# FFN2 of the second half as seven block products for eight of eighteen tile pairs, with attention's pieces dealt anew

## The chip, the cores and the metric

The kernel runs on one core of one Trainium2 chip. The metric is the device time of one execution in microseconds; each kernel is executed several times and the median counts. Five engines matter: PE (TensorE, matmuls, with PEld for its weight loads), DVE (VectorE), ACT (ScalarE), POOL (GpSimd) and SP (SyncE). In this kernel SP, ACT and POOL issue the DMA transfers.

## The reference

```
xn  = layernorm(x)                                   # x: 2048 tokens x 576
q, k, v = split(xn @ wqkv)                           # 32 heads of 18
attn[s, w] = softmax over w of q[s] . k[s - 2 w] / sqrt(18),   w = 0..7, s - 2 w >= 0
A   = (sum over w of attn[s, w] * v[s - 2 w]) @ wo
h   = relu(xn @ w1 + b1) ** 2                        # 4608 wide
B   = h @ w2 + b2
out = x + A + B                                      # all in fp32
```

## The kernel before, in words

**Tiles.** The 2048 tokens are four blocks b = 0 to 3 of 512. The 4608 columns of the hidden layer are 36 tiles of 128, taken in 18 pairs p. The 576 output features are five chunks, four of 128 and one of 64. Everything lies transposed: features in the partitions, tokens along the free axis.

**Precision.** An fp32 operand is split into a rounded part ("hi", written by ACT) and the rest ("lo", written by DVE), and a product is hi·hi + lo·hi + hi·lo. One tile of FFN2 in one block is 14 matmuls of 512 columns (`tile_products`, `add`): four chunks times three, and two for the chunk of 64, where hi and lo lie side by side. ACT therefore writes `w2s` (hi of w2) and `h` (hi), and DVE writes the lo of both, for every tile or pair.

**Stages.** `phase_a(0)` computes FFN1 of blocks 0 and 1 together, pair after pair (`ffn_pair`), by seven block products in Strassen's manner (the slots are named T1, B11, B22, B21, T3, T2, T4; `S1` to `S4` are sums of blocks of xn). Between its matmuls stand those of FFN2 of block 0. The squared hidden values of block 1 are stored in DRAM (`hscr`). `phase_b0` is FFN2 of block 1 from there, and then q, k and v of the second half ("quads", L1093). `phase_a(1)` and `phase_b1` do for blocks 2 and 3 what the first two did for 0 and 1. `tail` closes block 3. At the end of each block come five steps with `wo` (`o_ops`), whose operand is attention's output, loaded by `regroup` (`st<-o`, `r<-o`), transposed and split by `o_hi` and `o_lo`.

**Attention** runs on DVE, ACT and POOL beside the matmuls. A group of heads of a block is a generator of 19 pieces: four products with k and their four reductions in turn, the maximum, the exponential, sum and division, then four products with v and their four sums in turn. `side(k)` puts k pieces at the place in the program where it is called; `complete(b)` puts all that are left up to block b. Eight such generators run in the second half.

**Order.** Every engine executes its instructions in the order in which the code is written; the same holds for the three DMA queues. A piece of attention that stands ahead of a drain or a split on DVE is done first.

**What to look for.** FFN1's matmuls are at L661 and L667, FFN2's at L557; `w2_hi` at L530, `h_hi` at L989; `drain` adds a finished bank to the residual; all two-operand VectorE work goes through `tt`, L118 (L128 in the changed kernel). In the changed kernel FFN2's matmuls are at L590, those of the block products at L1514, `w2_hi` at L562, `o_hi` at L1011 and L1012, the sum and division of attention at L416 and L417.

Of the kernel before, what the change touches and what calls it, by code (L numbers as in the profile page):

```python
# [45 lines left out]
PIECES = (0, 0, 0, 2, 3, 4, 0, 3, 1, 0, 2, 2, 1, 0, 2, 2, 4, 5)  # L46
# [4 lines left out]
def block_kernel(ctx: ExitStack, tc: tile.TileContext, x, xt, wqkv, wo, w1, b1, w2, b2, w1l, out):  # L51
# [55 lines left out]
    lwscr = [dram.tile([G, 2, L, NS * P], F32, name=f"lw{i}") for i in range(-(-NP // G))]  # L107
    hscr = [[dram.tile([P, 2 * TB], F32, name=f"h{s}{p}") for p in range(NP)] for s in range(2)]
# [246 lines left out]
    def fetch():  # L355
        while free[0] > kept_back[0] and loads:
# [6 lines left out]
            t = landed[kind, b, g] = kv_tile(NE * CG + 32)[:, :NE * CG].rearrange("p (e c) -> p e c", c=CG)  # L363
            if kind == "k":
# [3 lines left out]
            lane[0].dma_start(t.rearrange("p e c -> p (e c)"),  # L368
                              flat(scr[kind][g], (PAD + b * TB - HALO) * CG, [NJ * CG, P], NE * CG))
# [58 lines left out]
    current = [None, None, None]  # L428

    def side(k, exp=True):  # L430

        while k > 0:
            if current[0] is None:
# [3 lines left out]
                current[:] = [make(), None, name]  # L437
            if current[1] == "exp" and not exp:
                return k
            try:  # L440
                current[1] = next(current[0])
                k -= 1
            except StopIteration:
                current[0] = None
        return 0

# [43 lines left out]
    def open_w1(n, k):  # L490
        w1s[n, k] = mt.tile([P, 2, 4, 2 * P], F32R, name="w1s", bufs=3)[:, :, :slots(n, k)]
# [18 lines left out]
    stream = [(b, n) for b in range(NB) for n in (*range(NF), *(f"o{c}" for c in range(NC)))]  # L510
# [11 lines left out]
    his, los = [0], [0]  # L522
# [9 lines left out]
    def w2_lo():  # L532
# [6 lines left out]
        load_w2(i + 3)  # L539
# [98 lines left out]
    def ffn_pair(s, p, work, first=False):  # L638
# [5 lines left out]
        stacked = p >= PLAIN  # L644
        A11 = lambda k, c: X[b0][:, k, c]
# [8 lines left out]
        def product(to, slot, a, start=False):  # L654
# [3 lines left out]
            if stacked:  # L658
                mm.append((LW[p % 2, slot], ST[slot]))
# [9 lines left out]
        def part(i):  # L669
# [9 lines left out]
            if i == 0 and p + 1 >= PLAIN and not last:  # L679
                load_left_weights(p + 1)  # L680
            if i == 0 and p == 1 and s:
                load_stack(1, sb.tile([P, 4, TB], F32R, name="w1r", bufs=2), 4)
# [33 lines left out]

        def finish_pair():
# [11 lines left out]
        if current[1] == "exp":  # L729
# [8 lines left out]
        if not first:  # L738
            side(2 + (p > 2) if s else PIECES[p], False)
# [10 lines left out]
        if before:  # L750
            next(before, None)

        def splits():
# [4 lines left out]
            if not own_w2:  # L758
# [3 lines left out]
            if not own_w2:  # L762
# [14 lines left out]
        elif not last:  # L777
            w1_hi(n + 1, 1)
            w1_lo(n + 1, 1)
        product(ba, B21, A12)  # L780
# [3 lines left out]
        work(2)  # L784

        def third():
            product(bc, B22, S4)
            left(bc, 1, x4["d"])
            if not first:
                part(1)  # L790
                side(2)
# [17 lines left out]
        else:  # L809
            third()  # L810
            h0 = square_hi(r0)
            square(r0)
            fourth()
        side(2, False)
        hs[n] = h0
        prev["r"] = r0, r1, h0
        prev["finish"] = finish_pair()
        work(3)

    def phase_a(s, filler):  # L820
# [3 lines left out]
        for p in range(1, NP):  # L824
            h, ops = hs.pop(s * NP + p - 1), []

            def work(i):
                if i in (0, 2):
                    ops.extend(tile_products(b, 2 * p - 2 + i // 2, h))
                add(b, ops[7 * i:7 * i + 7])  # L830

            if p == NP - 1:
# [7 lines left out]
        if s:  # L840
            residual(b)
        else:
# [5 lines left out]
        load_h(s, 0)  # L848
# [17 lines left out]
        load_h(s, 1)  # L866
        load_left(b)
        for c in range(NC):
            w2_hi()
            if c == 2:  # L870
                h_hi(s, 0)
            add(b, o_ops(b, c), range(NC) if c == NC - 1 else ())
# [7 lines left out]
        finish(b)  # L880
# [3 lines left out]
    def regroup(b, k):  # L884
        if b == 1:
            assert free[0]
# [913 lines left out]
```

## Time and profile before

| | us |
| --- | --- |
| median of 3 runs | 1105.33 (1104.26 to 1106.77) |
| the profiled execution | 1104.88 |
| its span | 1103.2 |
| TensorE granted clock | 1.0 in every stage |

The profiled execution is one of those runs, 0.4 us below their median; 1.7 us of it lie outside the span. The stages in the trace: `phase_a(0)` to about 430, `phase_b0` to about 660 (the quads in its last third), `phase_a(1)` to about 970, `phase_b1` and `tail` to the end.

### The profile page before, as it was taken

The page shows a single profiled execution, that of the slowest core. Times are in us where ns is not written, and L with a number is a line of the kernel's source. Part 1 is how long each engine was busy: PE and PEld are TensorE (multiplying, and loading weights), DVE is VectorE, ACT ScalarE, POOL GpSimd, SP SyncE. Part 2 cuts the span into 40 slices and gives each one's busy share as a digit, 9 for nine tenths or more (in the row PEclk, how much of TensorE's full clock was granted, in tenths as well). Part 3 has the DMA queues.
Part 4 walks back from the last instruction along what each step waited for, and adds up shares of the span by engine and source line. Part 5 has one row for each costly group of instructions (what it writes and reads, how often), then busy time and mean ns, then how long its engine had stood idle before and what let it go on. Part 6 is the DMA issues. An engine that isn't in the chain of part 4 may idle for free.

```text
span 1103.2 us, 13965 instructions
## 1 busy us (share of the span) xinstructions
PE 1091.4 (99%) x4919; PEld 918.8 (83%) x4919; DVE 889.3 (81%) x1197; ACT 566.5 (51%) x801; POOL 156.8 (14%) x284
## 2 busy tenths in 40 slices
PE   9999999999999999999999999999999999999998
PEld 7998888888888888888899887888888888888887
DVE  7996888999988979989899285776867676889955
ACT  5555655666656564555344354454554545543432
POOL 4011220212130100003010300202101010101010
PEclk9999999999999999999999999999999999999999
DMA  8768998897898697876865988868686877685582
GB/s 275 260 210 294 307 362 305 315 379 275 316 349 297 227 383 245 289 241 226 311 193 164 314 307 278 283 239 320 216 308 209 295 236 301 227 282 190 184 284 87
DMA packets 106549, 297.32 MB, mean 270 GB/s; under 512 B 12784, under 2 KB 39664, under 8 KB 95728
## 3 DMA queue, kind: packets, MB, share of 16 engines
q1 hardware_dynamic: 69104, 188.26, 49.1%
q0 software_dynamic: 14272, 67.24, 17.2%
q10 hardware_dynamic: 23104, 40.94, 11.1%
q8 instruction: 38, 0.62, 0.2%
q14 instruction: 31, 0.25, 0.1%
HBM read 211.90 MB, written 84.49 MB: 269 GB/s over the span
## 4 chain that ended last, share of the span: by engine, by line
PE 88%; DVE 6%; DMA 2%; issue 2%; ACT 1%; ACTq 1%; POOL 0%; DVEq 0%; POOLq 0%
PE p L557 45%; PE p L661 34%; PE p L1093 4%; DVE pr L118 2%; DMA w1s<-w 1%; PE p L1465 1%; PE p L1555 1%; PE p L1097 1%; DVE h L118 1%; DMA out<-h 1%; PE p L667 1%; PE p L1610 1%; DVE r L118 0%; PE p L1382 0%; DVE w1s L118 0%
## 5 line engine op out<-in xcount | busy, mean ns | idle before, releaser
L557 PE MATMUL p<-h,w2s 128*128 128x512 f32 x2066 | 491.9, 389 | 0.0
L557 PEld LDWEIGHTS p<-h,w2s 128*128 128x128 f32 x2066 | 387.6, 188 | 81.7 <-ACT h L708 0.5
L661 PE MATMUL p<-X,w1s 128*128 128x512 f32 x864 | 219.3, 389 | 0.0
L530 ACT ACTIVATE w2s<-w2r 128x640 fp32r<-128x640 f32 x164 | 120.3, 736 | 139.4 <-PE p L557 108.1
L661 PEld LDWEIGHTS p<-X,w1s 128*128 128x128 f32 x864 | 162.2, 188 | 33.7
L118 DVE TENSOR_TENSOR w2s<-w2r,w2s 128x576 fp32r<-128x576 f32 (+1 forms) x165 | 124.0, 752 | 77.2 <-ACT w2s L530 77.1
L661 PE MATMUL p<-S,w1s 128*128 128x512 f32 x648 | 164.8, 390 | 1.4 <-ACT r L746 1.4
L661 PEld LDWEIGHTS p<-S,w1s 128*128 128x128 f32 x648 | 121.5, 188 | 27.2 <-ACT r L746 1.8
L424 POOL DMA_DIRECT2D o<-q x128 | 69.5, 613 | 422.9 <-DVE q L118 421.8
L704 ACT ACTIVATE r<-r,b1t 128x512 f32<-128x512 f32 x72 | 52.2, 724 | 116.3 <-DVE r L118 113.6
L118 DVE TENSOR_TENSOR pr<-lg,kv 128x1152 f32<-128x1152 f32 x64 | 86.7, 1355 | 1.1
L395 DVE TENSOR_REDUCE lg<-pr 128x64 f32<-128x1152 f32 x64 | 86.5, 1351 | 1.2
L118 DVE TENSOR_TENSOR pr<-q,kv 128x1152 f32<-128x1152 f32 x64 | 86.7, 1354 | 0.9
L118 DVE TENSOR_TENSOR r<-p,r 128x512 f32<-128x512 f32 (+1 forms) x77 | 53.1, 690 | 35.5 <-ACT r L770 17.3
L118 DVE TENSOR_TENSOR pr<-pr 128x576 f32<-128x576 f32 (+1 forms) x128 | 77.6, 606 | 3.3
L712 ACT ACTIVATE r<-r 128x1024 f32<-128x1024 f32 x72 | 76.1, 1056 | 1.2
L746 ACT ACTIVATE r<-p 128x512 f32<-128x512 f32 x36 | 21.5, 598 | 84.2 <-PE p L661 81.1
L118 DVE TENSOR_TENSOR h<-r,h 128x1024 fp32r<-128x1024 f32 (+2 forms) x43 | 49.8, 1162 | 13.4 <-ACT r L712 9.6
L118 DVE TENSOR_TENSOR w1s<-w1r,w1s 128x1024 fp32r<-128x1024 f32 (+2 forms) x42 | 46.3, 1103 | 8.7 <-ACT w1s L495 8.2
L704 ACT ACTIVATE r<-p,b1t 128x512 f32<-128x512 f32 x72 | 48.2, 671 | 0.4 <-DMA out<-r 0.4
L118 DVE TENSOR_TENSOR h<-h 128x1024 fp32r<-128x1024 f32 x36 | 43.9, 1220 | 1.7 <-ACT h L989 1.5
L557 PE MATMUL p<-w1s,w2s 128*128 128x512 f32 x195 | 44.7, 389 | 0.0
(227 smaller groups left out, 1185.1 us busy)
## 6 DMA issues: line engine op xcount, KB each, us to landing
w2r<-in_w SPq DMA_DIRECT2D x144, 320.0 KB, 3.7
kv<-kvq POOLq DMA_DIRECT2D x32, 1296.0 KB, 8.2
w<-w1s SPq DMA_DIRECT2D x21, 1024.0 KB, 6.6
w1s<-w ACTq DMA_DIRECT2D x19, 1024.0 KB, 6.2
h<-r SPq DMA_DIRECT2D x36, 512.0 KB, 6.1
h<-h SPq DMA_DIRECT2D x36, 512.0 KB, 4.3
w<-w1s SPq DMA_DIRECT2D x15, 768.0 KB, 9.6
w1s<-w ACTq DMA_DIRECT2D x15, 768.0 KB, 5.6
```

The lines of the kernel that those rows point to most:

```text
L118: return nc.vector.tensor_tensor(out=out, in0=a, in1=b, op=op)
L395: nc.vector.tensor_reduce(out=lg[:, j * HG:(j + 1) * HG].rearrange("p a w -> p w a"), in_=pr.rearrange("p w (a d) -> p w a d", d=DH), axis ...
L424: nc.gpsimd.dma_start(rows[:, i], q[i * L:(i + 1) * L, :, a:z])
L530: nc.scalar.activation(w2s[stream[i]][:, :DE], raw2[i], AF.Copy)
L557: nc.tensor.matmul(yp[b][c], v, a, start=c not in yb[b], stop=c in last and c not in [o[0] for o in ops[i + 1:]], skip_group_check=True)
L661: nc.tensor.matmul(to, l, r, start=start and i == 0, stop=i == len(mm) - 1, skip_group_check=True)
L667: nc.tensor.matmul(to, weight(LEFT, k, f), v, start=False, stop=k == 1, skip_group_check=True)
L704: nc.scalar.activation(to, a, AF.Relu, bias=b1t[:, f:f + 1])
L712: nc.scalar.activation(r, r, AF.Square)
L746: nc.scalar.activation(u[:, 0], bb, AF.Copy)
L1093: nc.tensor.matmul(to, l[:, js], r, start=start and n == 0, stop=n == len(mm) - 1, skip_group_check=True)
L1097: nc.tensor.matmul(to, v[:, js], ws[LEFT, f][:, n], start=False, stop=n == 1, skip_group_check=True)
```

## The change

For the eight odd pairs 1, 3, ..., 15 (`PAIRED`), FFN2 of blocks 2 and 3 is done for both blocks at once by seven block products. The two-by-two blocks are: the two tiles of a pair against the two token blocks for h, and the two tiles against two halves of four chunks for w2.

- In `phase_a(1)` a paired pair isn't multiplied by w2. `finish_paired` forms its seven operands (squares and their sums and differences) and stores them in DRAM (`opscr`, 1.79 MB a pair). The matmuls of FFN2 of block 2 that remain, two tiles of ten pairs, are spread: one tile (14 matmuls) for each pair of FFN1 instead of two.
- A new `phase_blocks`, ahead of FFN2 of block 3, has 28 steps (`ORDER`). A step loads one operand of 512 KB, splits it two steps ahead, and does 12 matmuls, or 16 where the chunk of 64 goes along. The weights of the eight pairs come in four quadrants (`w2q`), are subtracted from each other in place (`turn_weights`) and split (`weights_hi`, `weights_lo`). Sums of banks go to the residual in between.
- FFN2 of block 3 has 20 tiles left: 18 in a loop, then five steps with wo, then two in `tail`.
- Attention's pieces are dealt by tables of numbers: `QUADS` in the quads, `SPOTS` in `phase_a(1)`, `LAST` in `phase_blocks`, `SINGLES` in the loop of block 3, one digit or count for each place.
- Left-over weights of FFN1 (`load_left_weights`) come two pairs ahead instead of one; the stack of left-over rows is loaded in pair 1 instead of in the quads; buffers for block 1's and block 3's attention output and residual change; k is loaded ahead of q.

```diff
+SPOTS = ('000001',) + ('110022', '110023', '110023', '110023') * 4 + ('110021',)
+QUADS = ('01111110111110', '10100010101011', '00110111111111', '10010000111111', ...)
+LAST = '0000000000000000001111111111'
+SINGLES = '12121212121200000000'
+PAIRED = tuple(range(1, 16, 2))
...
+        def finish_paired():
+            r1, t = prev.pop("r")
+            k = PAIRED.index(p)
+            y = mt.tile([P, 4, TB], F32, name="h", bufs=3)
+            nc.scalar.activation(y[:, :2], r1, AF.Square)
+            tt(t[:, 2], y[:, 0], y[:, 1], ALU.add)
+            tt(t[:, 3], t[:, 2], t[:, 0], ALU.subtract)
+            yield
+            nc.sync.dma_start(opscr[k // 2][:, k % 2, :4], t)
+            tt(y[:, 2], t[:, 1], t[:, 3], ALU.subtract)
+            tt(y[:, 0], t[:, 0], y[:, 0], ALU.subtract)
+            nc.sync.dma_start(opscr[k // 2][:, k % 2, 4:], y[:, :3])
+            yield
...
-                if n in ((1, 2, 3, 4, 5, 6, 8, 9, 10, 11, 12), (0, 2, 5, 6, 8, 10, 12, 13), (2, 3, 5, 6, 7, 8, 9, 10, 11, 12, 13), (0, 3))[2 * k + half]:
-                    side(1)
+                side(int(QUADS[2 * k + half][n]))
...
+    ORDER = ([(B11, A11S, g) for g in range(NG)] + [(T1, S1S, g) for g in range(NG)] +
+             [(T2, S2S, g) for g in range(NG)] + [(B21, A12S, g) for g in range(NG // 2)] +
+             [(T3, S3S, g) for g in range(NG)] + [(B21, A12S, g) for g in range(NG // 2, NG)] +
+             [(B22, S4S, g) for g in range(NG)] + [(T4, A22S, g) for g in range(NG)])
...
+    WHEN = {1: [(T1, 1)], 3: [(T2, 0)], 5: [(T2, 1)], 6: [(B21, 0)], 8: [(B21, 1)], 10: [(T3, 0)],
+            12: [(T3, 1)], 16: [(B22, 0)], 18: [(B22, 1)], 20: [(T4, 0)], 22: [(T4, 1)]}
...
+            operand_hi(k + 2)
+            for at in WHEN.get(k, ()):
+                weights_hi(*at)
+            operand_lo(k + 2)
+            for at in WHEN.get(k, ()):
+                weights_lo(*at)
...
+            if k == 19:
+                for c in range(2):
+                    tt(x2[:, c], aa[c], x2[:, c], ALU.add)
...
+            side(int(LAST[k]))
...
+                if len(xr[b]) < 2 and (m == 12 or not queue and current[0] is None):
+                    complete(b)
+                    regroup(b, 0)
+                    regroup(b, 1)
...
+                for c in {14: (0,), 15: (1,), 16: (2,), 17: (3,)}.get(m, ()):
+                    o_hi(b, c)
+                    o_lo(b, c)
+                side(int(SINGLES[m]))
```

**Where instructions move, 1.** VectorE of the changed kernel, from what follows step 19 of `phase_blocks` in the code to the end of step 20. The names: `S_7717<-p` adds banks to the residual of block 2, `xf` is the chunk of 64, `sm` and `lg` are a softmax piece, `X` is a weight quadrant turned, `h` the lo of operand 22 and `w1s` that of 21 and 23, `w1r` the lo of T4's weights.

```order
L128 TENSOR_TENSOR w1s<-w1s 128x1024
L128 TENSOR_TENSOR S_7717<-p_7900,S_7717 128x512
L128 TENSOR_TENSOR S_7717<-p_7901,S_7717 128x512
L1063 SCALAR_TENSOR_TENSOR xf<-p_5712,b2t,xf 64x512
L128 TENSOR_TENSOR xf<-p_5712,xf 64x512
L416 TENSOR_REDUCE sm<-lg 128x32
L417 RECIPROCAL sm<-sm 128x32
L128 TENSOR_TENSOR lg<-lg,sm 128x256
L128 TENSOR_TENSOR X_7719<-X_7719 128x1024
L128 TENSOR_TENSOR h<-h 128x1024
L128 TENSOR_TENSOR w1r<-X_7719,w1r 128x1024
L128 TENSOR_TENSOR pr<-lg,kv 128x1152
```

Before, FFN2 of block 3 stood here; three tiles of it put these rows on VectorE, with three pieces of attention (a product, its reduction, the maximum):

```order
L118 TENSOR_TENSOR h<-h 128x1024
L118 TENSOR_TENSOR pr<-q,kv 128x1152
L118 TENSOR_TENSOR w2s<-w2r,w2s 128x576
L395 TENSOR_REDUCE lg<-pr 128x8x8
L401 TENSOR_REDUCE mx<-lg 128x32
L118 TENSOR_TENSOR lg<-lg,mx 128x256
L118 TENSOR_TENSOR w2s<-w2r,w2s 128x576
L118 TENSOR_TENSOR h<-h 128x1024
```

The drains, the piece, the turn and the two splits now stand in one run, where one split of 576 or 1024 stood between pieces.

**Where instructions move, 2.** VectorE in FFN2 of block 3, from the last sums of attention (`q<-pr` is its output) to the first transposes for wo (`STREAM_TRANSPOSE`), before:

```order
L118 TENSOR_TENSOR q<-pr 128x144
L118 TENSOR_TENSOR w2s<-w2r,w2s 128x576 x2
L118 TENSOR_TENSOR h<-h 128x1024
L118 TENSOR_TENSOR w2s<-w2r,w2s 128x576 x2
L118 TENSOR_TENSOR h<-h 128x1024
L118 TENSOR_TENSOR w2s<-w2r,w2s 128x576 x2
L118 TENSOR_TENSOR h<-h 128x1024
L118 TENSOR_TENSOR w2s<-w2r,w2s 128x576 x2
L118 TENSOR_TENSOR h<-h 128x1024
L916 STREAM_TRANSPOSE r_8914<-st 128x512
```

and with the change:

```order
L128 TENSOR_TENSOR q<-pr 128x144
L128 TENSOR_TENSOR w2s<-w2r,w2s 128x576 x2
L128 TENSOR_TENSOR h<-h 128x1024
L1011 STREAM_TRANSPOSE r_8905<-st 128x512
L128 TENSOR_TENSOR w1s<-r_8905,w1s 128x512
L128 TENSOR_TENSOR w2s<-w2r,w2s 128x576
L1011 STREAM_TRANSPOSE r_8928<-st 128x512
L128 TENSOR_TENSOR w1s<-r_8928,w1s 128x512
L128 TENSOR_TENSOR w2s<-w2r,w2s 128x576
L128 TENSOR_TENSOR h<-h 128x1024
```

Eight tiles (one `w2s` each) lay between the last sum and the first transpose; two lie there now.

## Rows read from the trace of the kernel before

**Rows 1.** The page: the span, then each engine's busy time, share and instructions.
```profile
span 1103.2 us, 13965 instructions
...
PE 1091.4 (99%) x4919; PEld 918.8 (83%) x4919; DVE 889.3 (81%) x1197; ACT 566.5 (51%) x801; POOL 156.8 (14%) x284
```

**Rows 2.** Windows: stretch and us, then each engine busy, granted clock, DMA share, GB/s.
```profile
core 0: us, PE busy (x) PEld busy (x) DVE busy (x) ACT busy (x) POOL busy (x), PEclk, DMA share, GB/s
100.00:400.00 300.00, 299.96 (x1320) 247.30 (x1319) 265.86 (x384) 187.08 (x252) 58.29 (x100) 1.00 0.87 316
...
500.00:700.00 200.00, 194.44 (x906) 169.59 (x905) 153.34 (x198) 87.91 (x137) 29.38 (x53) 1.00 0.78 256
700.00:950.00 250.00, 250.00 (x1104) 207.09 (x1103) 175.80 (x217) 128.45 (x177) 28.31 (x53) 1.00 0.74 262
```

**Rows 3.** PE's timeline in FFN2 of block 3: start, us, instruction, count.
```profile
1035.81 36.43 PE L557 MATMUL p<-h,w2s 128*128 128x512 f32 x160
```

**Rows 4.** Timelines of 563 to 577, the quads; in brackets idle before and its releaser.
```profile
571.69 1.35 DVE L395 TENSOR_REDUCE lg<-pr 128x64 f32<-128x1152 f32 x1
572.95 1.05 DVE L118 TENSOR_TENSOR w1r<-w1r 128x864 f32<-128x864 f32 x1
...
574.03 0.92 ACT L1025 ACTIVATE w1s<-w1r 128x864 fp32r<-128x864 f32 x1 [3.28 <-DVE w1r L118]
574.87 0.94 ACT L1103 ACTIVATE kv<-p 128x432 f32<-128x432 f32 x2
...
575.43 1.08 PEld L1093 LDWEIGHTS p<-h,X 128*128 128x128 f32 x6 [1.28 <-ACT kv L1103]
```

**Rows 5.** DVE's timeline of 649 to 672, the end of block 1 and after.
```profile
650.01 2.48 DVE L118 TENSOR_TENSOR h<-p,h 128x512 f32<-128x512 f32 x4
652.41 1.40 DVE L118 TENSOR_TENSOR r<-p,r 64x512 f32<-64x512 f32 x2
...
668.98 0.41 DVE L406 TENSOR_REDUCE sm<-lg 128x32 f32<-128x256 f32 x1
...
670.27 1.36 DVE L118 TENSOR_TENSOR pr<-lg,kv 128x1152 f32<-128x1152 f32 x1
```

**Rows 6.** DVE's timeline of 1040 to 1049.5, the last pieces of attention.
```profile
1043.42 0.75 DVE L118 TENSOR_TENSOR w2s<-w2r,w2s 128x576 fp32r<-128x576 f32 x1
1044.09 1.22 DVE L118 TENSOR_TENSOR h<-h 128x1024 fp32r<-128x1024 f32 x1
1045.22 1.25 DVE L118 TENSOR_TENSOR pr<-pr 128x576 f32<-128x576 f32 x2
1046.50 0.31 DVE L118 TENSOR_TENSOR q<-pr 128x144 f32<-128x144 f32 x1
1046.73 1.42 DVE L118 TENSOR_TENSOR w2s<-w2r,w2s 128x576 fp32r<-128x576 f32 x2
```

**Rows 7.** POOL's timeline of 1036 to 1072: the stores of attention's output and `regroup`.
```profile
1047.11 4.33 POOL L424 DMA_DIRECT2D o<-q  x8 [35.86 <-DVE q L118]
1054.22 0.56 POOL L899 DMA_DIRECT2D st<-o  x1 [2.78 <-DMA o<-q]
```

**Rows 8.** DMA issues of 1040 to 1080: KB each and median us to landing.
```profile
h<-h SPq DMA_DIRECT2D x5, 512.0 KB, 4.8
...
st<-o POOLq DMA_DIRECT2D x1, 768.0 KB, 7.6
...
o<-q POOLq DMA_DIRECT2D x4, 48.0 KB, 4.0
```

**Rows 9.** Timelines of DVE and ACT where the first chunk for wo is transposed and split.
```profile
1068.34 0.70 DVE L916 STREAM_TRANSPOSE r<-st 128x512 f32<-128x512 f32 x1
...
1069.08 0.63 ACT L917 ACTIVATE w1s<-r 128x512 fp32r<-128x512 f32 x1 [1.91 <-DVE r L916]
1069.61 0.72 ACT L530 ACTIVATE w2s<-w2r 128x640 fp32r<-128x640 f32 x1
```

**Rows 10.** The chain that ended last (start, us), and PE's timeline at its end.
```profile
659.73 15.16 DMA w1s<-w
...
674.93 0.72 PE L667 MATMUL p<-x,w1s 128*128 128x512 f32 x2 [1.73 <-DMA w1s<-w]
```

**Rows 11.** DMA issues of 700 to 950: KB each and median us to landing.
```profile
w1s<-w ACTq DMA_DIRECT2D x13, 1024.0 KB, 5.5
...
st<-o POOLq DMA_DIRECT2D x1, 768.0 KB, 13.9
```

**Rows 12.** The page: DMA busy tenths and GB/s in 40 equal slices of the span.
```profile
DMA  8768998897898697876865988868686877685582
GB/s 275 260 210 294 307 362 305 315 379 275 316 349 297 227 383 245 289 241 226 311 193 164 314 307 278 283 239 320 216 308 209 295 236 301 227 282 190 184 284 87
```

More of the change, by code (lines that the diff above doesn't have):

```diff
@@ L445, in side, with some_side @@
         return 0
+    owed = [0]
+    def some_side(t):
+        owed[0] += t
+        while True:
+            exp = current[1] == "exp"
+            cost = COST[steps_done[0]] if current[0] is not None else COST[0]
+            if owed[0] < cost / 2 or side(1):
+                break
+            owed[0] -= cost
+            if exp or current[1] == "exp":
+                break
     def due(b):
@@ L508, in w1_again, with tiles @@
         queue.dma_start(open_w1(n, k).bitcast(F32), w1scr[n - NP][k])
-    stream = [(b, n) for b in range(NB) for n in (*range(NF), *(f"o{c}" for c in range(NC)))]
+    def tiles(b):
+        return range(NF) if b < 2 else [2 * p + f for p in SINGLE for f in range(2)]
+    stream = [(b, n) for b in range(NB) for n in (*tiles(b), *(f"o{c}" for c in range(NC)))]
     for c in range(NC):
@@ L644, in ffn_pair @@
         stacked = p >= PLAIN
+        paired = s and p in PAIRED
+        twice = not s or last
         A11 = lambda k, c: X[b0][:, k, c]
@@ L678, in part @@
                     load_two_rows(b, h)
-            if i == 0 and p + 1 >= PLAIN and not last:
-                load_left_weights(p + 1)
+            if i == 0 and not s and p + 1 >= PLAIN and not last:
+                load_left_weights(s, p + 1)
+            if i == 0 and s:
+                for q in range(PLAIN if p + 1 == PLAIN else p + 2, min(p + 3, NP) if p + 1 >= PLAIN else 0):
+                    load_left_weights(s, q)
             if i == 0 and p == 1 and s:
-                load_stack(1, sb.tile([P, 4, TB], F32R, name="w1r", bufs=2), 4)
+                for q in (0, 4):
+                    load_stack(1, sb.tile([P, 4, TB], F32R, name="w1r", bufs=2), q)
             if i == 2 and p == PLAIN - 1 and not s:
@@ L737, in ffn_pair, with spot @@
         part(0)
-        if not first:
-            side(2 + (p > 2) if s else PIECES[p], False)
+        def spot(i):
+            if s and (not first or i == 5):
+                some_side(int(SPOTS[p][i]))
+        if not first and not s:
+            side(PIECES[p], False)
+        spot(0)
         work(0)
@@ L810, in ffn_pair @@
             third()
-            h0 = square_hi(r0)
-            square(r0)
-            fourth()
[L814 to L817, printed above, removed]
+            if paired:
+                t = mt.tile([P, 4, TB], F32, name="h", bufs=3)
+                nc.scalar.activation(t[:, :2], r0, AF.Square)
+            else:
+                h0 = square_hi(r0)
+                square(r0)
+            fourth()
+        if not s:
+            side(2, False)
+        spot(5)
+        if paired:
+            prev["r"] = r1, t
+            prev["finish"] = finish_paired()
+        else:
+            hs[n] = h0
+            prev["r"] = r0, r1, h0
+            prev["finish"] = finish_pair()
         work(3)
@@ L865, in phase_a @@
         side(1)
-        load_h(s, 1)
+        if not s:
+            load_h(s, 1)
         load_left(b)
         for c in range(NC):
-            w2_hi()
-            if c == 2:
-                h_hi(s, 0)
-            add(b, o_ops(b, c), range(NC) if c == NC - 1 else ())
+            if s:
+                early_operands(c)
+            if his[0] < blocks_at:
+                w2_hi()
+            else:
+                held[1] += 1
+            if c == 2 and not s:
+                h_hi(s, 0)
+            add(b, o_ops(b, c), range(NC - s) if c == NC - 1 else ())
+            if s:
+                late_operands(c)
+                if los[0] < blocks_at:
+                    w2_lo()
+                continue
             w2_lo()
@@ L957, in open_left @@
     def open_left(b):
-        xr[b].append(four()[:, 0])
+        xr[b].append(four()[:, 0] if b < 2 else sb.tile([P, TB], F32, name="xf") if b == 2 else
+                     mt.tile([P, TB], F32, name="x41"))
     def load_left(b):
@@ L1245, in hook @@
                     w1_again(NP, 1, nc.sync)
-            if kept_back[0] and "last" in stage and not due(1):
+            if "last" in stage and (b, 0) not in ob and not due(1):
                 regroup(b, 0)
+                kept_back[0] = 0
                 fetch()
```

298 lines of the change are left out of this document (240 added, 58 removed).

## The prediction

> **What bounds the kernel now.** I began with the page's totals: TensorE is busy for 1091.4 of 1103.2 us, VectorE for 889.3, ScalarE for 566.5 [rows 1]. The reader should see two things there: a matmul saved is worth almost its full time, and VectorE is the next engine up, with about 214 us to spare over the span. The windows by stage then show that TensorE idles 0 us in 250 of the second `phase_a` (700 to 950), and 5.6 us in 200 around the quads [rows 2]; the clock is 1.00 in every window, so no term below is a matter of clock. The gaps of that stretch I followed one by one in the timelines: the two on which I lean are one of 1.28 us at 575.43, where a bank waits for ACT and ACT for VectorE [rows 4], and one of 1.73 us at 674.93, which the chain of waits puts on a load of FFN1 weights [rows 10]. One matmul of 512 columns costs 0.2267 us: a row of 160 lasts 36.43 us, the last of them 0.39 us alone, so (36.43 - 0.39) / 159 [rows 3].
>
> The sums below stand against the profiled execution, 1104.9 us (span 1103.2 and 1.7 around it); the median shown is 0.4 us higher.
>
> **1. Matmuls.** Removed: 2 blocks x 16 tiles x 14 = 448. Added: 28 steps x 12 = 336, and 4 more for the chunk of 64 in 16 of the steps, 64. Net 48 fewer, all of 512 columns: -48 x 0.2267 = **-10.9 us**. Seven products for eight save an eighth of 384 = 48, and the chunk of 64 costs what it did.
>
> **2. The stall at 575.** VectorE does a reduction of attention (1.35 us at 571.69) ahead of the step that ACT then waits 3.28 us for [rows 4]. The new table of the quads has no piece at that place (the sixth digit of its second row is 0, and the old tuple had 5). The chain moves forward by the piece less the 0.08 us by which neighbours overlap, about 1.27, at most the gap of 1.28; I take **-1.1**, bounds 0 (another wait follows) and -1.3. The piece goes to places where VectorE has room.
>
> **3. VectorE in steps 20 to 26 of the block stage.** The added VectorE work as a whole, 34 splits or turns of 1024 at 1.13, 46 adds of 512 at 0.62 less 32 splits of 576 at 0.67-0.75, is about 45 us net (38 + 29 - 22) [rows 5, 6], and VectorE stays under 90% of the span; a mean doesn't decide, so I went through the order. Ahead of the table's first 1 (step 18) the steps have 2 to 3 us of VectorE work for 2.7 to 3.6 us of matmuls. From step 19 the first fence of the change counts. The two adds wait for step 19's last matmul, so VectorE can't be ahead there. From that moment: adds 1.24 (half of 2.48), drains of the chunk of 64 1.40, a softmax piece 1.29 (668.98 to 670.27), the turn 1.13, operand 22's low part 1.22 [rows 5, 6], together 6.3, and 0.2 to start. TensorE meanwhile does steps 20 and 21, 24 matmuls = 5.44, and one with the high part, 5.67: wait 0.8. Each later step then has more VectorE work than matmuls: 3.55 (weights 1.13, product 1.28, operand 1.13) against 2.72, +0.8; 4.44 (w2 0.67, sums 1.51, turn 1.13, operand 1.13) against 2.72, +1.7; 4.21 against 3.63, +0.6; 3.88 against 3.63, +0.25. Sum **+4.2**. Below, 2.5 if half of the four later differences is taken up by pieces that come later than I read; above, 5.5 with 0.25 of latency at each of the five. Not 0: the drains and the piece stand where I counted them. One cover that could still give 0 is a residual add that doesn't have to wait for the end of step 19; then TensorE has 3.6 us more. So 0 is the outer bound.
>
> **4. The first transposes for wo.** In block 3 the last piece is now called in `complete` in tile 12 of the loop, and `o_hi` from tile 14 on; before, eight tiles lay between (the second place of the change). What `o_hi` waits for doesn't shrink: from the last sum on VectorE to the issue of `st<-o` POOL takes 4.33 us for eight stores and waits 2.78 us for their landing, 1046.81 to 1054.22 = 7.4; the load lands after 7.6 [rows 7, 8]. Counted from the start of tile 12: its splits end after 3.1, `complete`'s sums after 4.6, with 0.5 of lag since VectorE has 6.5 to 6.9 us for two tiles of 6.35; then 7.4 and 7.6: 20.1. Then the transpose, ACT's copy, and the high part of w2 that ACT has queued behind it, 2.0 from 1068.34 to 1070.33 [rows 9]: 22.1. That w2 is tile 17's (there are three buffers, ACT is two tiles ahead), and tile 17 is due after 70 x 0.2267 = 15.9. Wait 6.2, or 3.9 if the load lands in 5.1 because little else is moving. I take **+5.5**. Queued behind ACT's wait is only this split; behind VectorE's, the low parts of the same tiles.
>
> The Trainium skill ("DMA: Bandwidth & Descriptors", section "Anatomy of one DMA — SWDGE (gpsimd) path") has 2.0 us plus bytes over 436 GB/s for such a load, an estimate of 3.8 us for 768 KB, with which this wait would be about 2.4. The row has 7.6 and the same load took 13.9 in the busier stretch [rows 8, 11]; the row decides.
>
> **5. ACT in the second `phase_a`.** A pair is now 63 matmuls, 14.3 us, and ACT's work of FFN1 is what it was at 17.5. Where an even pair is followed by an odd one its list is tight: **+0.5**, bounds 0 and 2.
>
> **6. At nothing.** The operands' way through DRAM: they are stored 40 us and more ahead, and six loads of 512 KB are in flight, 4 steps = 10.9 us against a landing of 4.8 [rows 8]; without that cover, 28 x (4.8 - 2.7) = 59 us. `finish_paired` and the pieces in the second `phase_a`: 10.3 to 14.4 us of VectorE for a pair of 14.3, while `phase_a(0)` idled 0.04 us of 300 with VectorE at 265.9 [rows 2]. The load of block 2's attention output is issued 2.7 us into the last pair and lands within 13.9 [rows 11], 16.6 in all, its transposes are wanted at 19.4. The load order of k and q, the earlier left-over weights and the stack in pair 1 move transfers within a stage that has DMA to spare, if the next rival doesn't hold.
>
> Sum: 1104.9 - 10.9 - 1.1 + 4.2 + 5.5 + 0.5 = 1103.1; against the median **1103.5**.
>
> **Rivals.** *A, the forecast*: both waits come, 1100 to 1106.5 by their bounds.
>
> *B, one or both don't come*: 1097.6 without the one at tile 17, 1098.9 without that of the block steps, 1093.4 without either. For it: pieces of the last attention would end some tiles earlier if the pieces of the block stage got ahead by two or three, or stores of `o<-q` (4.0 us each [rows 8]) may overlap better in a quiet stretch. Against: both are counted in order, and the sums leave no slack above 2 us.
>
> *C, loads late in the second `phase_a`, slower*: the same number of bytes of FFN1 weights passes in 258.6 us instead of 317, and 1792 KB of operands for each paired pair are added. Adding up KB and counts of the code's transfers I get 86 MB in 18 pairs, so 336 GB/s; the same sum for 700 to 950 before gives 271 where the row has 262 [rows 2]. The first four pairs, with the stack and two pairs' left-over weights, want 22.8 MB in 57.6 us = 396. The page has 383 at most in a slice of 27.6 us [rows 12], and `phase_a(0)` ran at 316 for 300 us with TensorE idle 0.04. By 383: 59.5 us, +1.9; if 316 were the ceiling of the whole stage, 86 MB take 272, +13.4. So 1105 to 1116. It decides when `w1s<-w` lands more than 12.3 us after its issue (15.5 before, shrunk by 63 / 77): the median now is 5.5 [rows 11], but 15.16 on the chain at 660 [rows 10]. Against: the stores of operands, the largest addition, are wanted only in the block stage, and FFN1's weights have a queue of their own.
>
> The Trainium skill ("DMA: Bandwidth & Descriptors", section "Where 436 GB/s comes from") holds 358 GB/s to be what binds one core's traffic with HBM; by it the first four pairs would take 63.7 us, +6.1, so 1109. The trace doesn't bear out a hard limit there: three slices have 362, 379 and 383 [rows 12].
>
> *D, VectorE late in the second `phase_a`*: if each of the 8 paired pairs lost 0.5 us to splits that stand behind two pieces, +4, 1107.
>
> That the matmuls aren't fewer can't be: the counts are in the code.
>
> **How the numbers follow.** A 0.45, B 0.27, C 0.20, D 0.08. The likeliest is A, so 1103.5, its own range 1100 to 1106.5. For 8 in 10: up to 1111 leaves out about half of C (0.10), down to 1093.5 leaves out hardly more than the case without either wait (0.05): **1093.5 to 1111**. 0.2% is 2.2 us, about what a measurement can tell from no change, so "the same" is 1103.1 to 1107.5: faster is B and half of A, 0.27 + 0.22 + 0.01 = 0.50; the same is the other half of A and a part of D, 0.26; slower the rest of C and D, 0.24.
>
> **What would show it.** 4871 matmuls on the page. Gaps of TensorE ahead of block matmuls (L1514) in the steps after 21, of 0.8, 0.8, 1.7, 0.6 and 0.3 us, released by VectorE (`h`, `w1s`): right for 3. A gap of 4 to 6 us ahead of L590 near the end of the loop, with `r<-st` on VectorE waiting for the DMA of `st<-o`: right for 4. No gap at the bank that waited for `kv` in the quads: 2. Landings of `w1s<-w` above 12.3 us with TensorE released by that DMA would be C, and gaps released by VectorE (L128) ahead of L698 D. The forecast is wrong if steps 20 to 26 run in 2.72 and 3.63 us, or if the transposes find `st` landed.

## The result

The changed kernel takes 1110.47 us (median of 6 runs, 1109.56 to 1111.50) against 1105.90 (6 runs, 1104.26 to 1107.99): ratio 1.0039, 95% interval 1.0027 to 1.0051. It is slower by 0.4%. Forecast was no change, 1103.5, with faster at 0.50; the time lies inside the range, on the side that had 0.24.

The profiled execution took 1111.5 us. The page of the changed kernel, span and busy times:

```profile
span 1109.8 us, 13933 instructions
...
PE 1088.1 (98%) x4871; PEld 911.2 (82%) x4871; DVE 931.4 (84%) x1245; ACT 570.9 (51%) x800; POOL 160.3 (14%) x294
```

4871 matmuls against 4919 [rows 1], 48 fewer, as counted. The windows by stage of the changed kernel, columns as in [rows 2], cut at the places that the text speaks of:

```profile
core 0: us, PE busy (x) PEld busy (x) DVE busy (x) ACT busy (x) POOL busy (x), PEclk, DMA share, GB/s
500.00:640.00 140.00, 139.79 (x671) 125.66 (x671) 120.52 (x152) 63.72 (x102) 24.81 (x44) 1.00 0.76 263
...
660.00:675.00 15.00, 9.50 (x31) 7.28 (x30) 6.08 (x10) 3.00 (x5) 0.00 (x0) 0.77 1.02 330
...
690.00:900.00 210.00, 207.65 (x908) 168.69 (x908) 175.98 (x226) 109.85 (x156) 31.50 (x58) 1.00 0.90 335
...
990.00:1016.00 26.00, 23.75 (x101) 18.32 (x100) 24.25 (x30) 8.12 (x9) 0.00 (x0) 1.00 0.60 185
...
1073.00:1086.00 13.00, 7.39 (x22) 5.55 (x21) 6.64 (x10) 4.72 (x7) 0.54 (x1) 0.74 0.43 142
```

What to see: TensorE no longer idles in the quads, but in four other places; and in two of them, 660 to 675 and 1073 to 1086, the granted clock is 0.77 and 0.74 where every window before had 1.00.

Busy time hides what a slow matmul loses, so I added up, from the trace, the distance from each matmul's start to the next one's, less what it takes in rows without a wait, 0.2267 us (0.1955 for 432 columns). Lost time in us, by stretch:

| stretch | before | changed | difference | forecast |
| --- | --- | --- | --- | --- |
| start to 500 | 6.6 | 5.8 | -0.8 | 0 |
| quads, 500 to 640 | 5.2 | 0.7 | -4.5 | -1.1 |
| pairs 1 and 2 of the second `phase_a`, 640 to 690 | 2.1 | 8.6 | +6.5 | 0 |
| rest of it, 690 to 900 | 0.0 | 4.5 | +4.5 | +0.5 |
| wo of block 2 and steps 0 to 19, 900 to 990 | 0.1 | 0.4 | +0.3 | 0 |
| steps 20 to 27, 990 to 1016 | 0.0 | 3.5 | +3.5 | +4.2 |
| block 3, from 1016 | 0.0 | 8.4 | +8.4 | +5.5 |
| sum | 14.0 | 31.9 | +17.9 | +9.1 |

With 48 matmuls fewer, -10.9, and 0.4 us less behind the last matmul, this is +6.6, the difference of the two profiled executions (1111.5 - 1104.88). So nothing is left unexplained in size; the experiments are about causes.

**At 663.** The chain of waits of the changed kernel between 640 and 672 (start, us, what), and TensorE's timeline at its end:

```profile
646.05 8.40 DMA out<-h
...
654.53 14.67 DMA w1s<-w
...
669.24 1.22 PE p L704 x2
```

```profile
669.24 1.22 PE L704 MATMUL p<-x,w1s 128*128 128x512 f32 x2 [5.50 <-DMA w1s<-w]
```

It is the same load as in [rows 10]. Before it took 15.16 us and was waited for 1.73; now it takes 14.67 and is waited for 5.50. TensorE was ready for it 13.5 us after its issue before (674.93 - 1.73 - 659.73) and is ready after 9.2 now (669.24 - 5.50 - 654.53). I call this time the lead of the load. By the chain, the load is issued as soon as a store of block 1's output (`out<-h`) has landed, which took as long before (8.38 us).

**Steps 20 to 27.** TensorE's timeline of the changed kernel, rows with a wait in brackets:

```profile
999.47 2.79 PE L1514 MATMUL p<-w1s,S 128*128 128x512 f32 x11 [0.39 <-DVE w1s L128]
...
1003.92 1.43 PE L1514 MATMUL p<-h,w1r 128*128 128x512 f32 x5 [1.43 <-DVE h L128]
...
1008.26 1.43 PE L1514 MATMUL p<-w1s,w1r 128*128 128x512 f32 x5 [0.42 <-DVE w1s L128]
```

Each stands behind the first matmul of its step (steps 23, 24 and 25; start to start 0.55, 1.59 and 0.59 us too long, and 0.17 in step 26): the second one wants the low part of the operand. VectorE's timeline there is full, without an idle gap, from the drains to the last operand:

```profile
989.60 1.37 DVE L128 TENSOR_TENSOR S<-p,S 128x512 f32<-128x512 f32 x2 [0.83 <-PE p L1514]
990.89 0.73 DVE L1063 SCALAR_TENSOR_TENSOR xf<-p,b2t,xf 64x512 f32<-64x512 f32 x1
...
993.44 1.22 DVE L128 TENSOR_TENSOR X<-X 128x1024 f32<-128x1024 f32 x1
994.58 1.22 DVE L128 TENSOR_TENSOR h<-h 128x1024 fp32r<-128x1024 f32 x1
...
1001.51 1.22 DVE L128 TENSOR_TENSOR X<-X 128x1024 f32<-128x1024 f32 x1
1002.64 1.22 DVE L128 TENSOR_TENSOR h<-h 128x1024 fp32r<-128x1024 f32 x1
```

**Tile 17.** The timeline of the changed kernel, POOL, VectorE, ScalarE and TensorE:

```profile
1064.69 4.33 POOL L434 DMA_DIRECT2D o<-q  x8 [35.66 <-DVE q L128]
...
1072.44 0.56 POOL L994 DMA_DIRECT2D st<-o  x1 [3.42 <-DMA o<-q]
...
1077.08 0.71 DVE L1011 STREAM_TRANSPOSE r<-st 128x512 f32<-128x512 f32 x1 [10.09 <-DMA st<-o]
1077.82 0.63 ACT L1012 ACTIVATE w1s<-r 128x512 fp32r<-128x512 f32 x1 [12.09 <-DVE r L1011]
1078.36 0.72 ACT L562 ACTIVATE w2s<-w2r 128x640 fp32r<-128x640 f32 x1
...
1079.13 5.98 PE L590 MATMUL p<-h,w2s 128*128 128x512 f32 x14 [5.61 <-ACT w2s L562]
```

A wait of 5.6, the forecast's 5.5; and then 14 matmuls in 5.98 us instead of 3.34. That is the low clock: 0.427 us a matmul for eleven of them, the lower of the two levels, 1.2 GHz.

**In the second `phase_a`.** Two gaps, TensorE's timeline of the changed kernel:

```profile
795.32 1.66 PE L698 MATMUL p<-X,w1s 128*128 128x512 f32 x6 [1.47 <-DVE r L128]
...
802.95 1.43 PE L698 MATMUL p<-S,w1s 128*128 128x512 f32 x5 [0.54 <-ACT p L786]
```

and VectorE's ahead of the first:

```profile
785.91 1.42 DVE L128 TENSOR_TENSOR h<-h 128x512 f32<-128x512 f32 x2 [4.80 <-ACT h L762]
787.25 0.41 DVE L416 TENSOR_REDUCE sm<-lg 128x32 f32<-128x256 f32 x1
...
794.59 0.68 DVE L128 TENSOR_TENSOR r<-p,r 128x512 f32<-128x512 f32 x1
```

VectorE idles 4.8 us ahead of the operand adds of `finish_paired`, and then has the adds and four owed pieces of attention to do before the sum `r` that TensorE waits for.

### The profile page after: what moved, and what is told of

Same layout as the page of the kernel before. It is cut to its first block, busy times and chain, and to the rows that moved or that the text cites. A ratio compares the mean times of both kernels' runs of the same rounds, so it can differ in the third digit from the quotient of the medians.

```text
span 1109.8 us, 13933 instructions
## 1 busy us (share of the span) xinstructions
PE 1088.1 (98%) x4871; PEld 911.2 (82%) x4871; DVE 931.4 (84%) x1245; ACT 570.9 (51%) x800; POOL 160.3 (14%) x294
## 3 DMA queue, kind: packets, MB, share of 16 engines
q10 hardware_dynamic: 21184, 40.94, 10.9%
## 4 chain that ended last, share of the span: by engine, by line
PE 80%; DVE 10%; DMA 5%; issue 3%; ACT 1%; POOL 0%; SPq 0%; ACTq 0%; DVEq 0%; POOLq 0%
PE p L698 32%; PE p L590 29%; PE p L1187 7%; PE p L1514 6%; DVE pr L128 4%; PE p L1843 2%; DVE h L128 2%; PE p L1191 1%; DMA w1s<-w 1%; DVE w2s L128 1%; PE p L1898 1%; DMA op<-h 1%; PE p L704 1%; DMA out<-h 1%; PE p L1753 1%
## 5 line engine op out<-in xcount | busy, mean ns | idle before, releaser
L590 PE MATMUL p<-h,w2s 128*128 128x512 f32 x1618 | 392.6, 392 | 5.6 <-ACT w2s L562 5.6
L590 PEld LDWEIGHTS p<-h,w2s 128*128 128x128 f32 x1618 | 305.8, 189 | 71.2 <-ACT w2s L562 6.0
L698 PE MATMUL p<-S,w1s 128*128 128x512 f32 x648 | 167.3, 394 | 0.9 <-ACT p L786 0.9
L562 ACT ACTIVATE w2s<-w2r 128x640 fp32r<-128x640 f32 x132 | 96.7, 734 | 87.9 <-PE p L590 61.8
L128 DVE TENSOR_TENSOR w2s<-w2r,w2s 128x576 fp32r<-128x576 f32 (+1 forms) x133 | 99.7, 750 | 15.5 <-ACT w2s L562 15.5
L128 DVE TENSOR_TENSOR h<-h 128x1024 fp32r<-128x1024 f32 (+1 forms) x74 | 72.6, 989 | 23.2 <-ACT h L762 13.7
L128 DVE TENSOR_TENSOR r<-p,r 128x512 f32<-128x512 f32 (+2 forms) x81 | 55.0, 681 | 38.4 <-ACT r L831 20.3
L753 ACT ACTIVATE r<-r 128x1024 f32<-128x1024 f32 x56 | 59.2, 1057 | 0.9
L806 ACT ACTIVATE r<-p 128x512 f32<-128x512 f32 x36 | 21.6, 599 | 57.2 <-PE p L698 57.1
L831 ACT ACTIVATE r<-p 128x512 f32<-128x512 f32 x36 | 21.6, 600 | 56.4 <-PE p L698 56.4
L128 DVE TENSOR_TENSOR h<-r,h 128x1024 fp32r<-128x1024 f32 (+2 forms) x35 | 39.9, 1146 | 7.6 <-ACT r L753 6.0
```

Source lines behind the costliest of these rows:

```text
L128: return nc.vector.tensor_tensor(out=out, in0=a, in1=b, op=op)
L562: nc.scalar.activation(w2s[stream[i]][:, :DE], raw2[i], AF.Copy)
L590: nc.tensor.matmul(yp[b][c], v, a, start=c not in yb[b], stop=c in last and c not in [o[0] for o in ops[i + 1:]], skip_group_check=True)
L698: nc.tensor.matmul(to, l, r, start=start and i == 0, stop=i == len(mm) - 1, skip_group_check=True)
L753: nc.scalar.activation(r, r, AF.Square)
L806: nc.scalar.activation(u[:, 0], bb, AF.Copy)
```

## The experiments

Each experiment starts from the changed kernel; ratios are to the kernel before, run on the same chip. The changed kernel's own, repeated beside three of them, is the measure:

> The changed kernel itself, unaltered, for comparison beside the next three. All theories: 1.003 to 1.005 of the kernel before, the wait at 663 above 5 us and that at tile 17 between 3 and 6.

1110.50 us, ratio 1.0046 (1.0031 to 1.0060); 5.9 us too long at 664 and 5.2 at 1074, from one matmul's start to the next; 31.6 us lost in all, 6.7 of them from 1016 on.

**First transposes a tile later.**

```diff
-                for c in {14: (0,), 15: (1,), 16: (2,), 17: (3,)}.get(m, ()):
+                for c in {15: (0,), 16: (1,), 17: (2, 3)}.get(m, ()):
```

> The changed kernel with the first transposes for wo from tile 15 of block 3's loop on instead of tile 14 (the last two both in tile 17); nothing else differs. Theory (the wait at tile 17 is the way of attention's output to the transposes, and the low clock behind it comes with the length of the wait): the landing of st<-o stays where it is, the wait moves one tile back and shrinks by one tile, 3.2 us, from 5.8 to about 2.6, and the 2.6 us that the matmuls behind it lost at the granted clock of half speed go as well: about 1105, 5.8 us faster than the changed kernel. Rival (the low clock follows from the wait whatever its length): wait 2.6 and 2.6 of low clock, 1107.3. Rival (the wait is of something else that ACT or VectorE does before): no change, 1110.5.

TensorE's timeline of this kernel, and the window around it:

```profile
1079.21 3.49 PE L590 MATMUL p<-w1s,w2s 128*128 128x512 f32 x14 [1.89 <-ACT w2s L562]
...
1083.33 3.47 PE L590 MATMUL p<-w1s,w2s 128*128 128x512 f32 x14 [0.63 <-ACT w2s L562]
...
1088.05 2.33 PE L590 MATMUL p<-w1s,w2s 128*128 128x512 f32 x9 [1.25 <-ACT w2s L562]
```

```profile
1076.00:1090.00 14.00, 10.23 (x43) 7.47 (x42) 9.87 (x14) 5.98 (x9) 0.00 (x0) 1.00 0.28 86
```

The long wait fell from 5.61 to 1.89 and the clock stayed at 1.00; two short waits came behind it, which I put down to the transposes now following each other closely. From 1016 on 4.7 us are lost instead of 8.4 (6.7 in the control). The runs themselves can't show it: 1109.10 us against the 1105 expected, ratio 1.0045 (1.0031 to 1.0060), the same as the control's. What the trace says of this place is clear; what it is worth in time is not shown by this run alone.

**Pieces of the block stage earlier.**

```diff
-LAST = '0000000000000000001111111111'
+LAST = '0001000100000112110000000011'
```

> The changed kernel with the ten attention pieces of the block stage moved from steps 18 to 27 to steps 3, 7 and 13 to 17, and two left in 26 and 27. Theory (VectorE's list behind step 19 makes steps 21 to 26 wait, and it has 6 us free in steps 14 to 17): the gaps of 0.55, 1.59, 0.59 and 0.17 us go, 3.5 us with the small delays behind them, about 1107. Rival (the drains and turns alone are late, the pieces fill only idle time): no more than 1 us. The wait at tile 17 stays, since the last piece of all stands where it stood.

1104.92 us, ratio 1.0003 (0.9993 to 1.0013). Steps 20 to 27 lose nothing now; TensorE's timeline of this kernel in two of them:

```profile
998.78 2.88 PE L1514 MATMUL p<-w1s,S 128*128 128x512 f32 x12
1001.50 1.52 PE L1514 MATMUL p<-h,w1r 128*128 128x512 f32 x6
```

Twelve matmuls in 2.72 us from start to start, 16 in 3.63: VectorE's list was the cause, and the pieces were what made it too long.

The wait at tile 17 was expected to stay, and shrank from 5.61 us to 3.35 (at 1073.47). The last sum of attention comes 5.4 us into tile 12 here and 6.8 in the changed kernel, and `st<-o` is issued 7.2 us behind it instead of 8.0. So the full list seems also to have made attention's end late, and of the 4.8 us between this ratio and the control's some 3.5 belong to the steps and the rest to the end.

**Half of the stack in pair 2.**

```diff
-            if i == 0 and p == 1 and s:
-                for q in (0, 4):
-                    load_stack(1, sb.tile([P, 4, TB], F32R, name="w1r", bufs=2), q)
+            if i == 0 and p in (1, 2) and s:
+                load_stack(1, sb.tile([P, 4, TB], F32R, name="w1r", bufs=2), 4 * p - 4)
```

> The changed kernel with the second half of the stack of left-over rows (768 KB) loaded in pair 2 instead of pair 1. Theory (the load of w1s that TensorE waits for at 663 is slow because the stack, which the kernel before loaded half in the quads, runs beside it): it lands earlier, the wait of 5.5 us falls to 2 or less, its low clock goes, about 1104; the stack may be late for pair 3, then a new gap there. Rival (the lead is too short since a pair has 63 matmuls instead of 77, or other transfers are in the way): the wait stays above 4 us, 1109 to 1111.

The chain of waits of this kernel has the load, and TensorE's timeline its wait:

```profile
655.20 11.09 DMA w1s<-w
```

```profile
666.33 0.73 PE L704 MATMUL p<-x,w1s 128*128 128x512 f32 x2 [1.76 <-DMA w1s<-w]
```

The load lands 3.6 us sooner, the wait is 1.76, and the clock 1.00; from 640 to 690 2.2 us are lost instead of 8.6. But the 12 runs go from 1104.59 to 1112.58, the profiled one being the fastest: their median is 1108.54 us against the 1104 expected, ratio 1.0032 (1.0017 to 1.0047), which isn't told apart from the control's. The trace shows what the edit can do, not that it does it in most executions. The kernel before also had this second half of the stack in pair 1, and only the first half in the quads, so it is no transfer that the change had brought there.

**Left-over weights one pair ahead**, alone and later in the combined kernel (here pair 4's loads leave pair 2).

```diff
-                for q in range(PLAIN if p + 1 == PLAIN else p + 2, min(p + 3, NP) if p + 1 >= PLAIN else 0):
+                for q in range(p + 1, min(p + 2, NP) if p + 1 >= PLAIN else 0):
```

> The changed kernel with the left-over weights of FFN1 loaded one pair ahead as before, instead of two; pair 3's come in pair 2, so that two of the loads ahead of the wait at 663 (896 KB) go elsewhere. Theory (what runs beside w1s at 655 to 669 makes it late, and the left-over weights are a third of it): the wait at 663 falls by 2 us or more, 1106 to 1108.5. Rival (lead, not company): wait as it is, 1110.5, or later left-over weights make new gaps.

Ratio 1.0056 (1.0044 to 1.0068), and the wait is 5.18: as the rival has it. Of the 896 KB that I named only 448 had moved (`mb<-lw`; `st<-lw` stayed), so the theory had half of its test.

> The combined kernel with FFN1's left-over weights one pair ahead, as the kernel before had them; 448 KB less are issued beside the load of w1s that is waited for at 666. Theory (what is left of that wait, 2.4 us, is the company of these transfers): below 1 us there, 1.5 to 3 us faster in all. Rival (it is the load's own lead, which pairs of 63 matmuls shorten from 13.5 to 9 us): the wait stays above 1.7 us, time as the combined kernel's, ratio 0.992.

Ratio 0.9947 (0.9934 to 0.9961), above the combined kernel's 0.9921 (0.9902 to 0.9940, below). The chain and TensorE's timeline of this kernel:

```profile
647.03 9.63 DMA out<-h
656.73 13.29 DMA w1s<-w
```

```profile
670.07 1.22 PE L704 MATMUL p<-x,w1s 128*128 128x512 f32 x2 [5.36 <-DMA w1s<-w]
```

The wait is back at 5.36 us, 3.1 more than in the combined kernel: the lead is 8.0 instead of 9.2 us, since the store ahead of the load took 9.63 instead of 8.45, and the load took 13.29 instead of 11.34. The stack's second half now stood a place sooner in SP's queue; whether that is why isn't shown. So it isn't the number of bytes in the neighbourhood alone that decides, and neither theory covers this run: the rival had the wait above 1.7, but the time unchanged.

**The same transfers, more matmuls between issue and use.**

```diff
-                    cut = (0, 2, 6, 11, 14) if p % 2 else (0, 3, 7, 14, 14)
+                    cut = {1: (0, 0, 0, 8, 14), 2: (0, 10, 12, 14, 14)}.get(p, (0, 2, 6, 11, 14) if p % 2 else (0, 3, 7, 14, 14))
```

> The changed kernel with the same matmuls in another order in pairs 1 and 2 of the second phase_a: ten matmuls of FFN2 that stood ahead of the issue of the load of w1s that is waited for at 663, or behind its use, now stand between the two; no transfer is moved. Theory (the load takes 15 us in both kernels, 15.2 and 14.7, and what changed is its lead, 13.5 us before and 9.2 now): the lead grows by 10 x 0.2267 = 2.3 us, the wait falls from 5.2 to 5.9 to 3 to 3.6 us. Rival (the landing is tied to what is issued around it, so it moves back with the rest): the wait stays above 5 us.

The chain and TensorE's timeline of this kernel:

```profile
656.94 14.05 DMA w1s<-w
```

```profile
671.03 0.73 PE L704 MATMUL p<-x,w1s 128*128 128x512 f32 x2 [2.97 <-DMA w1s<-w]
```

```profile
660.00:675.00 15.00, 12.03 (x53) 9.66 (x52) 8.76 (x15) 5.05 (x9) 0.00 (x0) 1.00 1.02 303
```

The load takes about as long as it did, the lead is 11.1 us (671.03 - 2.97 - 656.94) instead of 9.2, the wait is 2.97, and the clock of 660 to 675 is 1.00. From 658 to 690 3.3 us are lost instead of the control's 8.9. 1107.22 us, ratio 1.0015 (1.0001 to 1.0028), below the control's 1.0046 (1.0031 to 1.0060). With the transfers as they were, the lead alone changes the wait: it is shown to be the cause of the wait's growth.

**A piece back in the quads.**

```diff
-QUADS = ('01111110111110', '10100010101011', ...
+QUADS = ('01111110111110', '10100100101011', ...
```

> The changed kernel with one piece of attention (a product, 1.35 us) put back from the seventh to the sixth place of the second row of the quads, where the kernel before had one. Theory (that piece makes ACT and then TensorE wait at 575): the gap before the bank there returns, 1 us or a little more, the time within 0.3% of the control's. Rival (the other moves in the quads removed the wait): gap below 0.3 us as in the changed kernel.

No wait came back. The matmuls that waited at 575.43 before are those at 573.67 here, and TensorE's rows follow each other:

```profile
572.50 1.33 PE L1187 MATMUL p<-w1s,S 128*128 128x432 f32 x6
573.67 1.38 PE L1187 MATMUL p<-h,X 128*128 128x432 f32 x6
```

Ratio 1.0044 (1.0027 to 1.0062). My theory, that the piece at the sixth place makes the wait, is refuted. The kernel before had pieces at the sixth and at the seventh place; this one has the sixth alone, the changed one the seventh alone. With two pieces ScalarE waited 3.28 us there [rows 4], with one it waits 2.15 here and 2.08 in the changed kernel. So the count seems to matter and not the place; but two pieces were never put into the changed kernel, so that isn't shown.

**The three edits together**, with 13 pieces in the block stage (`LAST = '0001000100000112110000003011'`), half of the stack in pair 2 and the transposes a tile later:

> The changed kernel with three edits: second half of the stack in pair 2, attention's pieces in the block stage at steps 3, 7, 13 to 17 and 24 to 27 (13 instead of 10), first transposes for wo from tile 15. Theory (three waits and two stretches of low clock make up all that was lost against the forecast by matmuls): -6.4 at 663, -3.5 in steps 21 to 26, -7 to -8.4 at the end: 1110.5 - 17 = 1093, ratio to the kernel before 0.986 to 0.990. Rival (the waits give way to others behind them, as transfers stay as dense): 1098 to 1104.

1096.39 us (1094.08 to 1099.65), ratio **0.9921 (0.9902 to 0.9940)**: 0.8% faster than the kernel before, 1.2% faster than the changed one. Its windows:

```profile
660.00:675.00 15.00, 12.78 (x50) 10.13 (x49) 9.79 (x16) 5.91 (x9) 0.00 (x0) 0.89 1.02 312
...
690.00:900.00 210.00, 207.07 (x906) 168.22 (x905) 175.08 (x226) 109.11 (x155) 31.43 (x58) 1.00 0.90 335
...
990.00:1094.00 104.00, 103.47 (x463) 85.75 (x461) 83.31 (x105) 37.56 (x48) 10.32 (x19) 1.00 0.59 191
```

Nothing is lost from 990 on. In its profiled execution 4.2 us remain at 666 and 5.1 in the rest of the second `phase_a`. The 4.2 are a wait of 2.22 us and some low clock behind it:

```profile
668.87 1.22 PE L704 MATMUL p<-x,w1s 128*128 128x512 f32 x2 [2.22 <-DMA w1s<-w]
```

It is 3 us short of the 1093 that I expected.

**Two variants on those remains.** First, at most two pieces at one place:

```diff
-        while True:
+        for _ in range(2):
```

> The combined kernel with at most two pieces of attention at a place of the second phase_a, where a debt of pieces had been worked off in threes. Theory (the gaps of 1.6 and 0.7 us at 793 and 802 are VectorE's, behind three pieces in a row): 2 us less than the combined one. Rival (they are ACT's or the transfers'): the same time.

Ratio 0.9955 (0.9939 to 0.9971), slower than the combined kernel; both gaps stay (1.64 and 0.70). The limit put one piece behind the second pair of adds, and the same four stood ahead of the sum. Second, the debt dropped behind an exponential, and `LAST = '0001000100000122210000003011'`:

```diff
             if exp or current[1] == "exp":
+                owed[0] = min(owed[0], 0)
                 break
```

> The combined kernel, in which the debt of pieces that builds up behind an exponential in the second phase_a is dropped, so that fewer pieces stand ahead of the sum that the matmuls at 793 wait for; five pieces more come in the block stage and its loop instead (two more at steps 14 to 16). Theory (that gap and the one at 802 are VectorE's, which idles 4.8 us ahead of the operand adds and then has them and the owed pieces ahead of the sum): both gaps below 0.4 us, 2 us less in the second phase_a; the last piece comes later, up to 2.5 us of wait may come back at the end. Rival (the gap is the operand adds' own, pieces or not): 1.6 and 0.7 as before.

The gaps are gone; TensorE's timeline of this kernel at the place:

```profile
789.18 1.75 PE L591 MATMUL p<-h,w2s 128*128 128x512 f32 x7
790.77 1.52 PE L699 MATMUL p<-X,w1s 128*128 128x512 f32 x6
```

690 to 900 loses 2.1 us instead of 5.1, but the pieces come back in the wo steps and the block stage (5.3 us from 900 to 1016) and at the end (5.5): ratio 0.9986 (0.9969 to 1.0002). The cause is shown; this is no way to use it.

**The stack's second half later still**, in the last third of pair 2.

```diff
-            if i == 0 and p in (1, 2) and s:
+            if (p, i) in ((1, 0), (2, 1)) and s:
```

> The combined kernel with the second half of the stack another 7 us later, in the last third of pair 2. Theory (whatever the stack's second half takes from the DMA engines while w1s is on its way is what w1s loses): the wait at 666, 2.4 us in the combined kernel, falls below 1.5 and its stretch of low clock goes, 2 us less; the half is wanted in pair 3 at about 680, a new gap there if it takes over 15 us. Rival (the rest of the wait is what the kernel before had at the same place, from the first half and the stores of block 1): 2 us stay.

TensorE's timeline of this kernel:

```profile
666.49 0.73 PE L704 MATMUL p<-x,w1s 128*128 128x512 f32 x2 [2.59 <-DMA w1s<-w]
...
683.09 0.47 PE L698 MATMUL p<-w1r,st 128*128 128x512 f32 x1 [1.57 <-DMA w1r<-stk]
```

Ratio 0.9921 (0.9894 to 0.9948), as the combined kernel. The rest of the wait isn't the second half's, which is now itself late (the 1.57 us at 683).

## Why the prediction was wrong

**Matmuls (-10.9)**: right, 4871.

**The stall at 575 (-1.1)**: it is gone. The chain moved forward by about one piece, as the term has it (ScalarE's wait went from 3.28 to 2.08 us), but the piece at the sixth place, put back alone, didn't bring the stall back, so the reason given is only in part borne out. The quads gained 4.5 (3.9 in the control), not 1.1. The gap ahead of `L746` at 627 went too, 1.5 us, which I had listed nowhere; at 542 the profiled executions of the changed kernel and of the variants with the same quads lose 0 to 0.9 where the one of before lost 1.3 (the run with the piece put back loses 1.2). What removed the gap at 627 wasn't tried.

**Steps 20 to 26 (+4.2)**: right, 3.5. In steps 23 to 26 the second matmul came 0.55, 1.59, 0.59 and 0.17 late, against 0.8, 1.7, 0.6 and 0.25 in the forecast; the first of the five, in step 22, didn't come.

**Tile 17 (+5.5)**: the mechanism is right, and the wait came to 5.6; that the number fits so well is luck. The last sum came 6.8 us into tile 12, not 5.1, the way from there to the issue of `st<-o` took 8.0, not 7.4, and `st<-o` landed after 4.6, not 7.6 [rows 8]. These +1.7, +0.6 and -3.0 bring the 6.2 computed down to 5.5, which is what I had picked between 6.2 and 3.9 without knowing any of them. The Trainium skill ("DMA: Bandwidth & Descriptors", section "Anatomy of one DMA — SWDGE (gpsimd) path") gives an estimate of 3.8 for this landing, nearer to the 4.6 than the row that I took. What failed here is the sentence that no term is a matter of clock: the matmuls behind this wait and behind the one at 663 ran at the low level, and this cost 2.6 us more at 1079 and 2.8 at 669. In the table, the changed kernel lost 8.8 us more than forecast: these 5.4, the 3.8 by which the wait at 663 grew, and 4.0 from 690 to 900, less 3.4 that the quads gained beyond the forecast; the other stretches make up the rest.

**At nothing**: this is the step that failed. I put the second `phase_a`'s loads at nothing and made their lateness a rival at 0.20, with the condition that `w1s<-w` lands more than 12.3 us after its issue. The row that shows it landing after 15.16 us, with TensorE waiting, stood beside that condition [rows 10]. (The 12.3 is also a slip: 15.5 x 63 / 77 is 12.7; the lead at this very place was 13.5, which scaled alike is 11.0.) The runs show 6.5 us lost there beyond what was lost before: 3.8 of wait and 2.8 of low clock. A load that is already waited for has no cover left: each microsecond by which matmuls between its issue and its use are taken away is added in full. Those were some 59 matmuls before and 41 now, 4.3 us less lead (13.5 to 9.2), and the wait grew by 3.8, from 1.73 to 5.50. Scaling by 63/77 missed it, since the matmuls taken out lay unevenly. The longer lead alone brought the wait down to 2.97, where 3 to 3.6 had been computed; sooner landing, in the one profiled execution with half of the stack away, brought it to 1.76 (14.7 to 11.1). So where the stack stands can count too. But it isn't what made the wait grow: the load took no longer than before, 14.67 against 15.16. Why it landed late again when the left-over weights of the combined kernel came one pair ahead stays open.

**Rival D**, VectorE in the second `phase_a`, came in small (2.3 us at 793 and 802; the forecast had +0.5 for ScalarE in this stage), not through the splits of every paired pair but through one debt of pieces behind an exponential. A further 0.5 us at 860 follows a row in which ScalarE waits 0.67 for a store of operands; I had not listed that the stores hold buffers, and no run tried it. The other 1.7 us of the 4.5 lie in gaps of 0.11 us and less.

**The bandwidth part of rival C**: the stage moved 335 GB/s, as computed (336), without TensorE waiting for a load after pair 2. Slices of the page (27.7 us each) reach 394 and 391 GB/s. Nothing here shows the 358 GB/s of the Trainium skill ("DMA: Bandwidth & Descriptors", section "Where 436 GB/s comes from") to be a limit for this core.

The range held the time because it reached to rival C; the likeliest case didn't.

## What to carry to other kernels

Where work is taken out of a stage, look first at every load on which the engine already waits, count the instructions between its issue and its use in both kernels, and add what is missing in full. After a wait of several microseconds look at the granted clock of the matmuls behind it, which cost half as much again as the wait here. Pieces that fill idle time belong where the list of their engine has room; ten of them moved to other steps gave back the 3.5 us that the steps of the block stage had lost. A forecast that hits a wait through terms that cancel isn't a check of the terms.

## What the runs showed that I had not expected

The granted clock fell to half, matmuls 0.427 us apart instead of 0.227, behind waits of 5.50 and 5.61 us (twelve and eleven matmuls), 5.36 (nine) and 2.22 (six), and stayed at 1.00 behind waits of 2.97, 2.59, 1.89 and 1.76. In the other profiles it fell behind every wait from 3.35 to 5.76 us, and behind waits of 2.40 and 2.73 in the kernel with the debt dropped. The length of the wait alone doesn't decide it: 2.22 had a low clock behind it and 2.97 had none.

The load of 1 MB, which lands after 5.5 us in the median between 700 and 950 in the kernel before [rows 11], took 11 to 15 us at 650 to 675 in every kernel, while the DMA engines were busy for 1.01 or 1.02 of the time of 660 to 675 and moved 303 to 389 GB/s.
